# Attention then a Winograd feed-forward: which engine subtracts for the low parts, and which one converts the weights

## The chip, the core and the metric

The kernel runs on one core of one Trainium2 chip. The metric is the device time of the whole program in microseconds (us), lower is better. Each kernel is given by the median of several executions; one more execution was recorded by the hardware profiler and left a trace.

## The reference, cut to what matters

First a linear attention over 8 batches, 8 heads, 576 positions and head width 64, with 128 random features; then a feed-forward layer on the 4608 tokens that result.

```python
def phi(x):
    proj = np.einsum('bhsd,df->bhsf', x, w_phi)
    proj = proj - np.max(np.abs(proj), axis=-1, keepdims=True)
    return np.concatenate([np.exp(proj), np.exp(-proj)], axis=-1)
q_p, k_p = phi(q), phi(k)
kv = np.einsum('bhsf,bhsd->bhfd', k_p, v)
z = np.sum(k_p, axis=2)
attn = np.einsum('bhsf,bhfd->bhsd', q_p, kv) / (np.einsum('bhsf,bhf->bhs', q_p, z)[..., None] + 1e-06)
x = attn.transpose(0, 2, 1, 3).reshape(4608, 512)
h = x @ w_in                                    # 512 x 2048
sp = np.where(h > 20.0, h, np.log1p(np.exp(np.minimum(h, 20.0))))
out = (h * np.tanh(sp)) @ w_out                 # 2048 x 512
```

All is fp32. The weights `w_in` and `w_out` reach the device as 64-bit words, and the kernel turns them into pairs of fp32 numbers itself: this is the weight conversion that the change is about.

## The kernel before, in words

**Attention.** It runs in 36 units of 512 (token, head pair) columns, for k and for q. Per unit TensorE (PE) projects into PSUM; VectorE (DVE) takes the maximum (L199) and subtracts it (L200); ScalarE (ACT) takes the exponentials; PE multiplies with v or with the sums; DVE divides (L304 to L306); PE transposes; ACT copies the result out of PSUM, and it is spilled to DRAM (`x_spill`).

**Feed-forward.** There are 72 steps. A step is 512 tokens (a segment, `s`) times 256 columns of the inner width (`fp`, 8 of them). Each step is seven products of one Winograd level, in two parts, `ff_in(n, 0)` with 24 matmuls and `ff_in(n, 1)` with 18 (L369), and the second layer of earlier steps, `ff_out`, twice 12 matmuls (L434). Every number goes through PE as a high and a low part in fp32r. So the operands are split:

- `x_load` fetches a segment's x into `x32` (one buffer), `x_sum` forms Winograd's differences (L344, on GpSimd, POOL), `x_block` makes seven blocks `xc`, the high part by a cast on ACT (L352) and the low part by a subtraction on DVE (L353).
- `winograd` (L381, L385, L389, L393, on DVE) adds the products in PSUM into `u`. The second part of `ff_in` overwrites what the first three read, so PE waits for L389 before its 18 matmuls.
- `mish` (ACT) applies the activation, `g_hi` casts the high part (L405, ACT), `g_lo` subtracts for the low part `gl` (L411, on POOL).

**Segments.** The first five groups of 512 tokens (`NFIRST`) are gone through with fp 0 and 1, then again with fp 2 and 3, in segments of two steps; all others in segments of four steps. A new segment needs its own x_load, x_sum and x_block.

**Weight conversion.** 32 pieces of 128 x 512 words ("in" or "out", fp, half k), in `weight_ops`. The first part works on bits: `absolute`, `clamp` (L115), `shift` (L119), `sign` (L123), `scale` (L129). The second is arithmetic: `low` (L133), then for "in" `total` (L145), four `sums` (L152), `hi` (a cast on ACT, L157) and `lo` (L161), and for "out" `hi`, `rest` (L166), `lo_out` (L170). All but `hi` and, for the first eight pieces, `absolute` run on DVE. The first eight pieces (fp 0 and 1) are converted during attention, the other 24 during the feed-forward. Those of fp 4 to 7 are spilled and loaded again when their turn comes.

**Order.** No scheduler decides: each action is entered with a nominal time by `at(time, ...)`, the list is sorted, and every engine gets its instructions in that order and executes them in that order. The conversion before is put into a list of free windows (`free`), each operation with a cost. `begin` is the nominal start of the feed-forward, `FFSTEP = 10.6` the nominal step.

Of the kernel before, what the change touches and what calls it, by code (L numbers as in the profile page):

```python
# [44 lines left out]
def attention_then_mish(ctx, tc, qT, kT, va, w_phi, w_in, w_out, out):  # L45
# [52 lines left out]
    def weight_ops(kind, fp, k, quiet):  # L98

        key = (kind, fp, k)  # L100

# [33 lines left out]
        def place():
# [200 lines left out]
    def x_sum(s, i):  # L336
        x32 = xT[s][0]
        if i == 0:
            xT[s].append(ffn.tile([P, 4, 2, CH], F32, tag="xs4", name=f"xs4_{s}", bufs=1))
# [4 lines left out]
        nc.gpsimd.tensor_tensor(o, a, b, op=ALU.subtract)  # L344
# [63 lines left out]
    def g_lo(n):  # L408
        gl = ffn.tile([P, 4, CH], F32R, tag="gl", name=f"gl_{n}", bufs=2)
        eng = nc.vector if n == len(steps) - 1 else nc.gpsimd  # L410
        eng.tensor_tensor(gl, u_live.pop(n)[3], g_live[n][0].bitcast(F32), op=ALU.subtract)  # L411
# [188 lines left out]
```

## Time and profile before

| what | value |
|---|---|
| median of 3 runs | 1144.0 us (1140.62 to 1147.89) |
| the profiled execution, its own time | 1138.37 us |
| its span, from first to last instruction | 1136.6 us |
| mean granted TensorE clock | 0.980 |
| busy: PE, DVE, ACT, POOL | 1064.7, 750.4, 493.7, 299.8 us |
| first h matmul of step 0 (start of the feed-forward) | 295.73 us |

The profile gives for each engine how long it was busy and which instruction ended its idle time. Shares over the whole span hide that this program has stages with different limits, so the stretches are looked at one by one: attention up to 296 us, and the feed-forward after it.

### The profile page before, as it was taken

The page shows a single profiled execution, that of the slowest core. Times are in us where ns is not written, and L with a number is a line of the kernel's source. Part 1 is how long each engine was busy: PE and PEld are TensorE (multiplying, and loading weights), DVE is VectorE, ACT ScalarE, POOL GpSimd, SP SyncE. Part 2 cuts the span into 40 slices and gives each one's busy share as a digit, 9 for nine tenths or more (in the row PEclk, how much of TensorE's full clock was granted, in tenths as well). Part 3 has the DMA queues.
Part 4 walks back from the last instruction along what each step waited for, and adds up shares of the span by engine and source line. Part 5 has one row for each costly group of instructions (what it writes and reads, how often), then busy time and mean ns, then how long its engine had stood idle before and what let it go on. Part 6 is the DMA issues. An engine that isn't in the chain of part 4 may idle for free.

```text
span 1136.6 us, 25710 instructions
## 1 busy us (share of the span) xinstructions
PE 1064.7 (94%) x11200; PEld 964.7 (85%) x11200; DVE 750.4 (66%) x1178; ACT 493.7 (43%) x811; POOL 299.8 (26%) x169
## 2 busy tenths in 40 slices
PE   7999999999888888888898999999999999999998
PEld 6899888998767777777787889999999999999997
DVE  4999999887668899899998863143244244244342
ACT  4667666666435355333333343243233233323331
POOL 0000000001134344433323323324324324324411
PEclk9999999999998899889998999999999999999999
DMA  4545545443223235545653521852320320320321
GB/s 146 188 149 163 191 137 171 131 142 128 71 84 111 93 112 176 176 183 188 201 201 104 200 71 41 300 185 109 112 76 37 111 87 26 112 94 20 110 74 38
DMA packets 64160, 143.45 MB, mean 126 GB/s; under 512 B 5040, under 2 KB 28720, under 8 KB 60464
## 3 DMA queue, kind: packets, MB, share of 16 engines
q1 hardware_dynamic: 64048, 141.81, 36.5%
q8 instruction: 88, 1.44, 0.5%
q14 instruction: 24, 0.20, 0.1%
HBM read 96.70 MB, written 45.09 MB: 125 GB/s over the span
## 4 chain that ended last, share of the span: by engine, by line
PE 47%; DVE 20%; issue 3%; ACT 2%; DMA 1%; POOL 0%; DVEq 0%; ACTq 0%; SPq 0%; POOLq 0%
PE h L369 24%; PE o L434 23%; DVE xc L353 2%; DVE w_in L152 2%; DVE w_in L145 1%; DVE w_in L119 1%; DVE u L393 1%; DVE t_in L133 1%; DVE w_out L123 1%; DVE w_in L123 1%; DVE wst_in L161 1%; DVE u L385 1%; DVE u L389 1%; DVE w_out L110 1%; DVE t_in L129 1%
## 5 line engine op out<-in xcount | busy, mean ns | idle before, releaser
L369 PEld LDWEIGHTS h<-xc,win 128*128 128x128 f32 x3024 | 390.5, 196 | 61.6 <-issue 18.1
L369 PE MATMUL h<-xc,win 128*128 128x256 f32 x3024 | 397.5, 288 | 46.0 <-DVE u L389 45.4
L434 PE MATMUL o<-wout,gh 128*128 128x512 f32 x1152 | 362.0, 396 | 2.9 <-ACT gh L405 2.9
L411 POOL TENSOR_TENSOR gl<-u,gh 128x1024 fp32r<-128x1024 f32 x71 | 173.3, 2441 | 512.2 <-ACT gh L405 450.8
L434 PEld LDWEIGHTS o<-wout,gh 128*128 128x128 f32 x1152 | 210.4, 192 | 39.8 <-ACT gh L405 3.1
L434 PE MATMUL o<-wout,gl 128*128 128x512 f32 x576 | 226.0, 392 | 1.9 <-POOL gl L411 1.7
L344 POOL TENSOR_TENSOR xs<-x 128x512 f32<-128x512 f32 x46 | 64.4, 1399 | 307.3 <-DMA x<-x_spill 282.4
L374 ACT COPY p<-h 128x256 f32<-128x256 f32 x72 | 26.8, 373 | 265.9 <-PE h L369 265.9
L381 DVE TENSOR_TENSOR u<-h,p 128x256 f32<-128x256 f32 x72 | 30.4, 422 | 167.5 <-ACT p L374 167.5
L434 PEld LDWEIGHTS o<-wout,gl 128*128 128x128 f32 x576 | 109.4, 190 | 27.4 <-POOL gl L411 3.2
L393 DVE TENSOR_TENSOR u<-h,u 128x512 f32<-128x512 f32 x72 | 49.4, 686 | 107.1 <-ACT u L398 104.1
L398 ACT ACTIVATE u<-h 128x256 f32<-128x256 f32 x72 | 27.6, 384 | 153.6 <-PE h L369 145.8
L353 DVE TENSOR_TENSOR xc<-x,xc 128x512 fp32r<-128x512 f32 x69 | 75.0, 1114 | 23.9 <-ACT xc L352 23.9
L208 PE MATMUL kvps<-v,e_k 128*64 128x65 f32 x2560 | 83.2, 224 | 5.0 <-ACT e_k L238 4.2
L208 PEld LDWEIGHTS kvps<-v,e_k 128*64 128x64 f32 x2560 | 79.5, 140 | 6.2 <-ACT e_k L238 4.7
L208 PE MATMUL num<-kv,e_q 128*64 128x65 f32 x2304 | 77.6, 223 | 2.6 <-ACT e_q L282 2.4
L208 PEld LDWEIGHTS num<-kv,e_q 128*64 128x64 f32 x2304 | 71.1, 137 | 8.6 <-ACT e_q L282 4.1
L405 ACT CAST gh<-u 128x1024 fp32r<-128x1024 f32 x72 | 75.6, 1050 | 2.2
L282 ACT ACTIVATE e_q<-dt 128x512 f32<-128x512 f32 x144 | 75.1, 612 | 0.1
L237 ACT ACTIVATE e_k<-e_k 128x1024 f32<-128x1024 f32 x36 | 38.1, 1058 | 78.6 <-DVE e_k L200 78.6
L344 POOL TENSOR_TENSOR xs<-x,xs 128x512 f32<-128x512 f32 x46 | 63.9, 1389 | 1.8
L353 DVE TENSOR_TENSOR xc<-xs,xc 128x512 fp32r<-128x512 f32 x92 | 63.2, 718 | 1.0 <-ACT xc L352 1.0
(60 smaller groups left out, 1113.1 us busy)
## 6 DMA issues: line engine op xcount, KB each, us to landing
x<-x_spill SPq DMA_DIRECT2D x46, 512.0 KB, 5.6
o_part<-part SPq DMA_DIRECT2D x14, 1024.0 KB, 4.8
part<-o_part SPq DMA_DIRECT2D x14, 1024.0 KB, 7.5
v<-va SPq DMA_DIRECT2D x32, 325.0 KB, 3.4
kraw<-kT SPq DMA_DIRECT2D x36, 256.0 KB, 3.9
qraw<-qT SPq DMA_DIRECT2D x36, 256.0 KB, 3.9
x_spill<-xs SPq DMA_DIRECT2D x36, 256.0 KB, 2.7
out<-part SPq DMA_DIRECT2D x36, 256.0 KB, 2.0
```

Source lines behind the costliest of these rows:

```text
L208: nc.tensor.matmul(ps[rows], lhsT[:, rows], rhs[h], start=start, stop=stop, skip_group_check=True)
L237: nc.scalar.activation(e[:, :, 1, :], e[:, :, 0, :], AF.Exp)
L282: nc.scalar.activation(e[:, s, :], ps, AF.Exp, scale=2.0 * s - 1.0)
L344: nc.gpsimd.tensor_tensor(o, a, b, op=ALU.subtract)
L353: nc.vector.tensor_sub(blk[:, 1], src, blk[:, 0].bitcast(F32))
L369: nc.tensor.matmul(ps, w, x, start=(i in (0, 2) and m == 0), stop=(m == 5), skip_group_check=True)
L381: nc.vector.tensor_tensor(u2, ps[:, 0, 1], u_live[n][0], op=ALU.add)
L393: nc.vector.tensor_tensor(u[:, 1:3], ps[:, 1], u2.unsqueeze(1).broadcast_to([P, 2, CH]), op=ALU.add)
L398: nc.scalar.activation(u[:, 0], h_live[n][:, 0, 0], AF.Mish)
L405: nc.scalar.copy(gh, u_live[n][3])
L411: eng.tensor_tensor(gl, u_live.pop(n)[3], g_live[n][0].bitcast(F32), op=ALU.subtract)
L434: nc.tensor.matmul(ps, g, w, start=(first and f == k == 0), stop=(last and f == 1 and k == 2))
```

## The change

Three things. (1) `gl` (L415 in the changed file) and the four differences of x per segment (L349) run on VectorE. The third difference is now written in place into `x32`, so that their tile has three slots instead of four. (2) In the weight conversion VectorE keeps the operations on bits; the arithmetic part (`sums`, `lo`, `rest` and `lo_out` in the same manner as `total` below) runs on GpSimd. There `low` becomes two instructions, a multiplication by a constant into the unused half of `w8` (L135) and a product (L137). The pieces are no longer put into free windows but follow each other at fixed distances: the operations on bits 5.0 ahead of the arithmetic, and between pieces a pause of EARLY = 22.0 during attention, SOON = 0.0 for the eight pieces of fp 2 and 3, LATER = 9.0 for the other 16. (3) `NFIRST` is 4 instead of 5, which makes 22 segments of 23; the steps stay 72. Beside these, the tile `wst` moves to another pool, the tile `xs` has two buffers of three, and within the feed-forward `x_block` and `gl` stand 1.4 and 0.9 later in nominal time.

```diff
+EARLY, SOON, LATER = 22.0, 0.0, 9.0
-NFIRST = 5
+NFIRST = 4
...
     def weight_ops(kind, fp, k, quiet):
+        eng = nc.gpsimd
...
         def low():
+            f = piece[key][1][:, 4:8].rearrange("p b m -> p (b m)")
+            nc.gpsimd.tensor_scalar(f, piece[key][0][:, 0], 2.0 ** -52, None, op0=ALU.mult)
             t = piece[key][2]
-            nc.vector.scalar_tensor_tensor(t, piece[key][0][:, 0], 2.0 ** -52, t, op0=ALU.mult, op1=ALU.mult)
+            nc.gpsimd.tensor_tensor(t, f, t, op=ALU.mult)
...
         def total():
-            nc.vector.tensor_tensor(w(), w(), piece[key][2], op=ALU.add)
+            eng.tensor_tensor(w(), w(), piece[key][2], op=ALU.add)
...
     def x_sum(s, i):
...
-        o, a, b = ((t1, b12, b11), (t2, b22, t1), (t3, b22, b12), (t4, b21, t2))[i]
-        nc.gpsimd.tensor_tensor(o, a, b, op=ALU.subtract)
+        o, a, b = ((t1, b12, b11), (t2, b22, t1), (b12, b22, b12), (t4, b21, t2))[i]
+        nc.vector.tensor_tensor(o, a, b, op=ALU.subtract)
...
     def g_lo(n):
-        eng = nc.vector if n == len(steps) - 1 else nc.gpsimd
-        eng.tensor_tensor(gl, u_live.pop(n)[3], g_live[n][0].bitcast(F32), op=ALU.subtract)
+        nc.vector.tensor_tensor(gl, u_live.pop(n)[3], g_live[n][0].bitcast(F32), op=ALU.subtract)
...
-    window, clock = 0, free[0][0]
+    clock = 6.0
     for i, pc in enumerate(pieces):
-        at(clock - 9.0, weight_load, *pc)
-        for cost, op in weight_ops(*pc, i >= 4 * 2):
-            while clock + 0.5 * cost > free[window][1]:
-                window += 1
-                clock = free[window][0]
+        quiet = i >= 8
+        if i == 8:
+            clock = max(clock, begin + 5.0)
+        at(clock - 12.0, weight_load, *pc)
+        bits, sums = weight_ops(*pc, quiet)
+        for delay, op in bits:
+            at(clock - 5.0 + delay, op)
+        for cost, op in sums:
             at(clock, op)
             clock += cost
+        clock += EARLY if i < 8 else SOON if i < 16 else LATER
```

The order shows what this does to the queues. First VectorE in attention, about the second piece. Before, the operations of one piece stand between those of the units, and go on over several units (w_in and t_in are the piece, m, e, pp of the attention unit):

```order
L123 SCALAR_TENSOR_TENSOR w_in_1_978<-words_in_1_741,w_in_1_978 128x512
L129 TENSOR_SCALAR t_in_1_1048<-w_in_1_978 128x512
L199 TENSOR_REDUCE m_k_1078<-pp_k_1057 128x8
L200 TENSOR_TENSOR e_k_1077<-pp_k_1057,m_k_1078 128x2x512
L133 SCALAR_TENSOR_TENSOR t_in_1_1048<-words_in_1_741,t_in_1_1048 128x512
L145 TENSOR_TENSOR w_in_1_978<-w_in_1_978,t_in_1_1048 128x512
```

Of the changed program, the same piece on VectorE:

```order
L117 TENSOR_SCALAR w_in_1_847<-w_in_1_847 128x512
L204 TENSOR_REDUCE m_q_894<-pp_q_787 128x8
L205 TENSOR_TENSOR e_q_893<-pp_q_787,m_q_894 128x2x512
L121 TENSOR_SCALAR w_in_1_847<-w_in_1_847 128x512
L125 SCALAR_TENSOR_TENSOR w_in_1_847<-words_in_1_746,w_in_1_847 128x512
L131 TENSOR_SCALAR t_in_1_906<-w_in_1_847 128x512
```

These four are all of the piece that VectorE still does in attention; the arithmetic stands on GpSimd, which has nothing else there.

Second, VectorE in steps 2 to 4 of the feed-forward, before: most of one piece stands between the last block xc, the adds u of step 4, and the piece's end.

```order
L353 TENSOR_TENSOR xc_6_5592<-xs_2_5448,xc_6_5592 128x512
L115 TENSOR_SCALAR w_in_1_5513<-w_in_1_5513 128x512
L119 TENSOR_SCALAR w_in_1_5513<-w_in_1_5513 128x512
L123 SCALAR_TENSOR_TENSOR w_in_1_5513<-words_in_1_5424,w_in_1_5513 128x512
L129 TENSOR_SCALAR t_in_1_5600<-w_in_1_5513 128x512
L133 SCALAR_TENSOR_TENSOR t_in_1_5600<-words_in_1_5424,t_in_1_5600 128x512
L145 TENSOR_TENSOR w_in_1_5513<-w_in_1_5513,t_in_1_5600 128x512
L381 TENSOR_TENSOR u_4_5635<-h_5602,p_4_5628 128x256
L385 TENSOR_TENSOR u_4_5639<-h_5602,u_4_5635 128x256
L389 TENSOR_TENSOR u_5657<-h_5602,u_4_5639 128x256
L152 TENSOR_TENSOR w_in_1_5513<-w_in_1_5513 128x128 x4
L161 TENSOR_TENSOR win_5481<-w_in_1_5513,win_5481 128x896
```

Of the changed program, VectorE from the adds of step 3 on: gl, one piece's five operations on bits, and the blocks xc between them. The differences of x (L349, four) stand in the step before and in the one after.

```order
L386 TENSOR_TENSOR u_3_5534<-h_5505,p_3_5530 128x256
L390 TENSOR_TENSOR u_3_5538<-h_5505,u_3_5534 128x256
L394 TENSOR_TENSOR u_5553<-h_5505,u_3_5538 128x256
L415 TENSOR_TENSOR gl_5556<-u_5456,gh_5536 128x1024
L112 TENSOR_SCALAR w_in_0_5559<-words_in_0_5500 128x512
L358 TENSOR_TENSOR xc_0_5563<-x_2_5436,xc_0_5563 128x512
L117 TENSOR_SCALAR w_in_0_5559<-w_in_0_5559 128x512
L121 TENSOR_SCALAR w_in_0_5559<-w_in_0_5559 128x512
L358 TENSOR_TENSOR xc_1_5569<-xs_2_5466,xc_1_5569 128x512
L125 SCALAR_TENSOR_TENSOR w_in_0_5559<-words_in_0_5500,w_in_0_5559 128x512
L358 TENSOR_TENSOR xc_2_5593<-xs_2_5466,xc_2_5593 128x512
L131 TENSOR_SCALAR t_in_0_5597<-w_in_0_5559 128x512
```

Third, GpSimd in the same steps, before: the last difference of segment 2, gl of two steps, and the first differences of segment 3.

```order
L344 TENSOR_TENSOR xs_2_5448<-x_2_5417,xs_2_5448 128x512
L411 TENSOR_TENSOR gl_5521<-u_5438,gh_5517 128x1024
L411 TENSOR_TENSOR gl_5641<-u_5535,gh_5637 128x1024
L344 TENSOR_TENSOR xs_3_5664<-x_3_5632 128x512
L344 TENSOR_TENSOR xs_3_5664<-x_3_5632,xs_3_5664 128x512
```

Of the changed program: one "in" piece, and the first instructions of the next. The last of a piece waits for its cast `hi` on ScalarE.

```order
L135 TENSOR_SCALAR w_in_0_5559<-words_in_0_5500 128x512
L137 TENSOR_TENSOR t_in_0_5597<-w_in_0_5559,t_in_0_5597 128x512
L149 TENSOR_TENSOR w_in_0_5559<-w_in_0_5559,t_in_0_5597 128x512
L156 TENSOR_TENSOR w_in_0_5559<-w_in_0_5559 128x128 x4
L165 TENSOR_TENSOR win_5694<-w_in_0_5559,win_5694 128x896
L135 TENSOR_SCALAR w_in_1_5688<-words_in_1_5600 128x512
L137 TENSOR_TENSOR t_in_1_5719<-w_in_1_5688,t_in_1_5719 128x512
```

By the order of the changed program VectorE has, from the adds of step 2 to those of step 8: 24 adds, 5 gl, 12 differences, 21 blocks xc and the operations on bits of 8 pieces; from step 8 to step 16: 32 adds, 8 gl, 16 differences, 28 blocks, 12 drains (L446, PSUM added to a tile) and the bits of 4 pieces. GpSimd has the arithmetic of 4 "in" and 4 "out" pieces in the first stretch, of 4 "in" and 1 "out" in the second.

More of the change, by code (lines that the diff above doesn't have):

```diff
@@ L160, in lo @@
             dst = piece[key][3]
-            nc.vector.tensor_sub(dst[:, 1], piece[key][1][:, 1:8], dst[:, 0].bitcast(F32))
+            eng.tensor_sub(dst[:, 1], piece[key][1][:, 1:8], dst[:, 0].bitcast(F32))
             done()
@@ L165, in rest @@
             dst = piece[key][3]
-            nc.vector.tensor_sub(w(), w(), dst[:, 0].bitcast(F32))
+            eng.tensor_sub(w(), w(), dst[:, 0].bitcast(F32))
         def lo_out():
             dst = piece[key][3]
-            nc.vector.tensor_tensor(dst[:, 1], w(), piece[key][2], op=ALU.add)
+            eng.tensor_tensor(dst[:, 1], w(), piece[key][2], op=ALU.add)
             done()
@@ L177, in done @@
                 nc.sync.dma_start(in_spill[fp, k] if kind == "in" else out_spill[fp, k], dst.bitcast(F32))
-        ops = [(0.42 if quiet else 0.1, absolute), (0.42, clamp), (0.42, shift), (0.69, sign), (0.42, scale), (0.69, low)]
+        ops = [(0.0, absolute), (0.9, clamp), (1.35, shift), (1.8, sign), (2.5, scale)]
+        rest_ops = [(2.2, low)]
         if kind == "in":
-            ops += [(0.69, total)] + [(0.29, lambda i=i: sums(i)) for i in range(4)] + [(1.1, hi), (1.08, lo)]
+            rest_ops += [(1.45, total)] + [(0.65, lambda i=i: sums(i)) for i in range(4)] + [(1.6, hi), (2.3, lo)]
         else:
-            ops += [(0.7, hi), (0.69, rest), (0.69, lo_out)]
-        return ops
+            rest_ops += [(1.3, hi), (1.45, rest), (1.45, lo_out)]
+        return ops, rest_ops
     def project(raw, name):
@@ L530, in attention_then_mish @@
         for i in range(4):
-            at(t + 5.5 + 1.2 * i, x_sum, s, i)
+            at(t + 5.5 + 0.7 * i, x_sum, s, i)
         t = t_of(n - 1) if n >= AHEAD + 2 else begin - (30, 3.9)[s]
         for b in range(7):
-            at(t + 3.5 + 0.8 * b, x_block, s, b)
+            at(t + (4.9 if n >= AHEAD + 2 else 3.5) + 0.8 * b, x_block, s, b)
     for n, (s, sc, fp, first, last) in enumerate(steps):
@@ L547, in attention_then_mish @@
         at(after + 1.8, g_hi, n)
-        at(after + 2.8, g_lo, n)
+        at(after + (3.7 if n >= AHEAD else 2.8), g_lo, n)
         out_a = (begin + 0.9, t_of(n + 1) + 2.8, t_of(n + 1) + 7.8)[min(n, 2)]
```

24 lines of the change are left out of this document (6 added, 18 removed).

## The prediction

> **What bounds the kernel now.** I read the page's busy slices first, then the stretches, then who waits for whom, then the rows of single steps.
>
> ```profile
> span 1136.6 us, 25710 instructions
> PE   7999999999888888888898999999999999999998
> DVE  4999999887668899899998863143244244244342
> ```
>
> PE (TensorE) is near full almost everywhere; the weak slices are 8 to 22, and there DVE (VectorE) is full too. From slice 23 on DVE is far from full. So I cut the span where a step of the feed-forward begins:
>
> ```profile
> 326.38 0.40 PE L369 MATMUL h<-xc,win 128*128 128x256 f32 x2
> 406.69 0.28 PE L369 MATMUL h<-xc,win 128*128 128x256 f32 x1
> 513.07 0.40 PE L369 MATMUL h<-xc,win 128*128 128x256 f32 x2
> 672.06 0.40 PE L369 MATMUL h<-xc,win 128*128 128x256 f32 x2
> ...
> 199.00:256.00 57.00, 57.00 (x1348) 54.27 (x1344) 46.78 (x79) 38.50 (x62) 0.00 (x0) 1.00 0.44 137
> 326.40:406.70 80.30, 67.33 (x386) 60.41 (x385) 66.61 (x94) 34.19 (x59) 30.73 (x17) 0.89 0.31 106
> 406.70:513.10 106.40, 89.98 (x530) 80.21 (x529) 97.86 (x137) 43.72 (x75) 43.50 (x24) 0.94 0.47 167
> 513.10:672.10 159.00, 142.19 (x860) 126.49 (x859) 144.97 (x216) 59.44 (x98) 55.92 (x29) 0.97 0.47 161
> 672.10:1124.40 452.30, 452.30 (x2839) 410.12 (x2838) 165.99 (x274) 153.62 (x255) 153.74 (x83) 1.00 0.27 97
> ```
>
> The first four rows are the first matmuls of steps 2, 8, 16 and 29. The others give, per stretch, its length and the busy time of PE, weight load, DVE, ACT, POOL (GpSimd), then the granted clock. After 672 us PE is busy without a gap: a step has 66 matmuls, 2839 / 66 = 43 steps in 452.3 us, **10.52 us a step**. At that rate steps 2 to 7 would take 63.1 us (they take 80.3), 8 to 15 84.2 (106.4), 16 to 28 136.8 (159.0): 61.6 us are lost, all while weights are being converted, with DVE busy 83%, 92% and 91%. What PE waits for:
>
> ```profile
> PE h L369 <- DVE u L389: 45.4, 13, 5.6
> 344.61 4.18 PE L369 MATMUL h<-xc,win 128*128 128x256 f32 x18 [4.67 <-DVE u L389]
> ```
>
> 13 waits for the third add of DVE; after such a gap the 18 matmuls run slower as well (the granted clock is 0.89 to 0.97 in these stretches, 1.00 after them). DVE bounds them, with its own work and with something else:
>
> ```profile
> 646.25 1.42 POOL L344 TENSOR_TENSOR xs<-x 128x512 f32<-128x512 f32 x1 [1.00 <-DMA x<-x_spill]
> 647.75 1.36 POOL L344 TENSOR_TENSOR xs<-x,xs 128x512 f32<-128x512 f32 x1
> 649.07 1.48 POOL L344 TENSOR_TENSOR xs<-x 128x512 f32<-128x512 f32 x1
> 650.51 1.47 POOL L344 TENSOR_TENSOR xs<-x,xs 128x512 f32<-128x512 f32 x1
> 655.40 2.41 POOL L411 TENSOR_TENSOR gl<-u,gh 128x1024 fp32r<-128x1024 f32 x1 [3.41 <-ACT gh L405]
> ...
> 646.44 1.52 DVE L110 TENSOR_SCALAR w_out<-words_out 128x512 uint32<-128x512 uint32 x1
> 648.00 1.40 DVE L115 TENSOR_SCALAR w_out<-w_out 128x512 f32<-128x512 f32 x1
> 649.43 1.40 DVE L119 TENSOR_SCALAR w_out<-w_out 128x512 uint32<-128x512 uint32 x1
> 650.75 0.68 DVE L393 TENSOR_TENSOR u<-h,u 128x512 f32<-128x512 f32 x1
> 655.87 2.48 DVE L353 TENSOR_TENSOR xc<-x,xc 128x512 fp32r<-128x512 f32 x1 [0.23 <-ACT xc L352]
> 658.27 1.88 DVE L353 TENSOR_TENSOR xc<-xs,xc 128x512 fp32r<-128x512 f32 x3
> 663.09 0.41 DVE L110 TENSOR_SCALAR w_out<-words_out 128x512 uint32<-128x512 uint32 x1
> 663.54 0.43 DVE L115 TENSOR_SCALAR w_out<-w_out 128x512 f32<-128x512 f32 x1
> 664.00 0.43 DVE L119 TENSOR_SCALAR w_out<-w_out 128x512 uint32<-128x512 uint32 x1
> 664.46 0.69 DVE L123 SCALAR_TENSOR_TENSOR w_out<-words_out,w_out 128x512 uint32<-128x512 uint32 x1
> 665.19 0.43 DVE L129 TENSOR_SCALAR t_out<-w_out 128x512 uint32<-128x512 uint32 x1
> ```
>
> The same operations take 0.41, 0.43, 0.43 us with POOL idle and 1.52, 1.40, 1.40 while POOL runs: one of DVE for one of POOL. A block xc that takes 0.63 (three in 1.88) took 2.48 beside a gl. The add L393, with an input in PSUM, kept its 0.68. So **each us of POOL costs DVE part of a us** where DVE works from SBUF: 3.05 of 4.26 us (0.72) over the first three, 1.85 of 2.41 (0.77) over the gl; DVE isn't always at such an operation, so I take two thirds of POOL's busy time. It fits: without it (20.5 of 66.6) DVE would have had 46 us in steps 2 to 7.
>
> The Trainium skill, "SBUF — State Buffer", section "Who interferes with whom", states this as a lock: whichever of the two issues first holds the shared ports for its whole instruction and the other fully blocks, and a VectorE operation with two inputs in SBUF is among those concerned. The trace agrees (2.48 against 0.63 us). By that rule gl and the differences of x come under the lock too once they are on VectorE, which speaks against that part of the change.
>
> **The change, part by part.** In **attention** the unit's rhythm can be read from one row per unit (units 2, 22 and 30 of 36):
>
> ```profile
> 39.45 1.21 DVE L199 TENSOR_REDUCE m_q<-pp_q 128x8 f32<-128x1024 f32 x1
> 200.49 1.21 DVE L199 TENSOR_REDUCE m_q<-pp_q 128x8 f32<-128x1024 f32 x1
> 260.19 1.21 DVE L199 TENSOR_REDUCE m_q<-pp_q 128x8 f32<-128x1024 f32 x1
> ```
>
> Up to 200 us, with eight pieces converted on DVE, a unit takes 161.04 / 20 = 8.05 us; after them 59.70 / 8 = 7.46, with PE busy for all of the stretch 199 to 256 and DVE for 46.78 of 57.00. Twenty units at the faster rate save 11.8 us. Four operations on bits stay, 0.43 + 0.43 + 0.69 + 0.43 = 2.0 us a piece, 16 us in all. DVE has 10.2 us free in 8 units, 1.3 a unit, but a piece's four come close together; I let each of the eight bursts cost PE 0.35 us. POOL's arithmetic beside it hits little: DVE's inputs there are in PSUM. **-9 us** (bounds -12 and 0). The sums of x for the first two segments (2.5 us each) fall into the tail of attention and cost nothing there as long as DVE waits for PE; without that cover 5.
>
> For the feed-forward I need prices on the other engine:
>
> ```profile
> L411 DVE TENSOR_TENSOR gl<-u,gh 128x1024 fp32r<-128x1024 f32 x1 | 1.2, 1226 | 2.0 <-ACT gh L405 2.0
> L385 DVE TENSOR_TENSOR u<-h,u 128x256 f32<-128x256 f32 x72 | 30.5, 424 | 2.5
> masks.py:199 POOL TENSOR_SCALAR_AFFINE_SELECT ident<-ident 128x128 f32<-128x128 f32 x1 | 0.3, 292 | 0.1
> 687.99 2.40 POOL L411 TENSOR_TENSOR gl<-u,gh 128x1024 fp32r<-128x1024 f32 x1 [8.12 <-ACT gh L405]
> 690.35 1.29 POOL L344 TENSOR_TENSOR xs<-x 128x512 f32<-128x512 f32 x1
> x<-x_spill SPq DMA_DIRECT2D x46, 512.0 KB, 5.6
> ```
>
> On DVE: a gl 1.23; the four adds of a step 3 x 0.42 + 0.68 = 1.96; a difference of x like a block xc of its size, 0.63; a drain like L393, 0.68; the bits of a piece 0.41 + 0.43 + 0.43 + 0.69 + 0.43 = 2.39. On POOL 512 columns take 1.29 and 1024 2.40, so 128 about 0.46 and 896 about 2.12. The multiplication by a constant (L135) isn't in the trace: at least the 0.29 of the 128-column select, at most the 2.40 of the 1024 columns, since its input skips every second word of 1024; I take 1.29, the row of its width. An "in" piece is then 3 x 1.29 + 4 x 0.46 + 2.12 = 7.8 us of POOL, an "out" piece 4 x 1.29 = 5.2.
>
> The Trainium skill, "GPSIMD Engine Reference", section "Engine selection", advises VectorE for elementwise work and calls one-input operations on GpSimd roughly line-rate. Its section "Elementwise — side-by-side cycle accounting" has 769 ns for a tight loop over 512 elements; estimated from that page L135 would take 0.77, and the sum below would be 5 us less. No run here shows it yet.
>
> - **Steps 2 to 7** (eight pieces, no pause between them). DVE: 6 x 1.96 + 5 x 1.23 + (12 + 21) x 0.63 + 8 x 2.39 = 57.8. POOL: 4 x 7.8 + 4 x 5.2 = 52.0, two thirds of it on DVE: 34.7. DVE idled 13.7 us here before, partly for casts that now stand on POOL's side; a difference of x now waits on DVE for its DMA (5.6 us from issue, and the issue waits for the last block of the segment before), which I put at 1 us a segment: 8 idle. Sum 100.5 against 80.3: **+20 us**.
> - **Steps 8 to 15** (four "in", one "out"). DVE: 8 x 1.96 + 8 x 1.23 + (16 + 28) x 0.63 + 12 x 0.68 + 4 x 2.39 = 71.0; POOL 36.4, of it 24.3; idle 6 (8.5 before). Sum 101.3 against 106.4: **-5 us**.
> - **Steps 16 to 28.** Eight pieces, three segments: DVE 13 x (1.96 + 1.23) + 33 x 0.63 + 4 x 0.68 + 8 x 2.39 = 84, plus two thirds of POOL's 52: 119 of PE's 136.8. PE bounds, but in the three steps that carry seven blocks (7.6 us with adds and gl) bits and POOL's lock come on top, 13 us against 10.52: 7 us lost instead of 22.2. **-15 us**.
> - **From step 29 on** PE was busy throughout and stays so: 0. That POOL frees DVE there is hidden by PE.
>
> Sum: -9 + 20 - 5 - 15 = **-9 us**. The profiled execution took 1138.4 us in all (1136.6 of span and 1.8 around it), so 1129.4; it lay 0.5% below the median of the runs, 1144.0, and with that ratio I say **1135 us**. About 1% is what a measurement of this kernel can tell from no change.
>
> **The rivals.**
>
> A. *The lock costs little.* POOL's instructions are shorter (0.46 to 2.1 instead of 2.4) and its chain waits for bits and casts; were one third of POOL's time to fall on DVE, steps 2 to 7 take 83 (+3), 8 to 15 89 (-17), the third stretch -18, attention -12: -44, **1100 us**. Against it: the three ratios above.
>
> B. *Attention gains nothing.* The bursts of bits make PE wait as the whole pieces did: -9 becomes 0, the sum 0, **1144 us**. For it: a burst of 2.0 us exceeds the 1.3 that a unit has free; against it: units without conversion run at 7.46.
>
> C. *Slower: DVE and POOL in lockstep.* In steps 2 to 7 POOL's pieces follow without pause and nearly all of DVE's new work there is from SBUF: 33 differences and blocks, 5 gl, 40 on bits. If every us of POOL falls on DVE, steps 2 to 7 take 118 (+38), 8 to 15 113 (+7), the third stretch -10, attention -9: +26, **1170 us**. Each tenth of the share is 5.2 + 3.6 us; the gain is gone at 0.77, and from 0.9 on the kernel is slower by over 1%. For it: the 0.72 and 0.77 are close; against it: POOL pauses for each cast on ACT. The Trainium skill's rule above (first come, the other fully blocks) describes this case.
>
> **How the numbers follow.** Forecast 0.47, A 0.15, B 0.18, C 0.20. Range 1108 to 1165: A's and C's far halves, 0.08 and 0.11, stay outside; the unknown L135, at 0.29 or 2.40, moves the forecast by 14 us down (21 pieces x 1.00 x 2/3) or 10 up (the 13 pieces up to step 15 x 1.11 x 2/3), inside it. Faster by over 1%: A and under half of the forecast, 0.36. Within 1%: the rest of the forecast, most of B, the near end of C, 0.42. Slower: 0.22.
>
> **What would show it.** Right: units of about 7.5 us up to 200 us; steps 2 to 7 about 100 us with DVE near 92% busy and POOL over 50; steps from 16 on at 10.5 us but for some; xc or gl on DVE far above 0.63 and 1.23 where POOL runs. Wrong: a unit of 8 us (B); steps 2 to 7 at 85 or 115 (A, C); L135 far from 1.3; PE waiting for POOL's weights at step 8; ACT held by a cast that waits for POOL, with its copy p behind it.

## The result, and the profile after

The changed kernel takes **1110.4 us** (median of 4 runs, 1109.84 to 1111.28) against 1144.06 (1140.62 to 1147.89): ratio 0.9706, 95% interval 0.9674 to 0.9738. It is 34 us faster; forecast were 9. The profiled execution took 1111.28 us, its span is 1109.5. The two traces differ by less than the medians, 27.1 us in span (1136.6 and 1109.5): of the kernel before, an execution 0.5% under the median was profiled, and of the changed kernel the longest of the four. All stretches below are of the traces.

The first lines of the page, the busy slices of PE, DVE and POOL (GpSimd):

```profile
span 1109.5 us, 25630 instructions
...
PE   7899999999888889999999999999999999999998
...
DVE  4788878888858987898846757545545545545543
...
POOL 0222211111027766543425443000000000000000
```

PE's weak slices are now 11 to 15 (11 to 20 and 22 before), and POOL is busiest just there and behind. The stretches are cut at the first matmul of steps 2, 8, 16 and 29 again; the columns are the length, then busy PE, weight load, DVE, ACT, POOL and the granted clock. The first row is a part of attention:

```profile
57.00:199.00 142.00, 138.92 (x3256) 130.69 (x3254) 120.43 (x205) 95.36 (x153) 32.49 (x31) 1.00 0.48 155
...
329.60:411.60 82.00, 68.45 (x386) 59.32 (x385) 71.83 (x93) 36.39 (x63) 57.69 (x45) 0.92 0.35 122
411.60:504.10 92.50, 86.42 (x529) 76.52 (x528) 79.48 (x122) 40.55 (x69) 47.46 (x37) 0.99 0.53 189
504.10:645.10 141.00, 138.18 (x859) 123.78 (x858) 98.85 (x148) 55.07 (x91) 61.39 (x49) 1.00 0.37 127
645.10:1097.40 452.30, 452.30 (x2839) 410.08 (x2838) 234.91 (x372) 154.94 (x258) 19.24 (x13) 1.00 0.29 103
```

Steps 2 to 7 take 82.0 us (80.3 before), 8 to 15 92.5 (106.4), 16 to 28 141.0 (159.0), and from 29 on a step still takes 10.52. So the whole gain of the trace lies in steps 8 to 28: 13.9 + 18.0 us. Step 0 starts at 297.7 us (295.7), so attention gained nothing. PE's wait for the third add, 45.4 us before, is now

```profile
L374 PE MATMUL h<-xc,win 128*128 128x256 f32 x3024 | 392.3, 285 | 20.2 <-DVE u L394 11.9
```

The lock that the prediction rests on can be added up from the rows of DVE: of each instruction its duration less the shortest of the same line and shape. This **excess** is 25.1, 11.0 and 17.2 us in the three stretches, 0.42, 0.23 and 0.28 of POOL's busy time there (59.0, 48.2 and 61.4 us, summed over its rows). Before the change it was 21.0, 28.9 and 37.6 us, 0.68, 0.66 and 0.67 of POOL's. (An instruction of DVE begins some 0.07 us before the one ahead of it has ended, so the durations of its rows add up to more than its busy time: 77.8 us for 71.8 in steps 2 to 7.)

Of the 87.5 us before, 42.7 lay on the operations on bits, 31.9 on the arithmetic and 12.4 on the blocks xc. Now bits have 9.6, nearly all of it in steps 2 to 7, blocks 24.8, and the differences and gl 17.8. So the conversion, which bore most of the lock before, now bears little of it. Why the share fell can be read in one stretch of a piece, POOL's rows first, then DVE's (start, duration):

```profile
383.76 1.87 POOL L135 TENSOR_SCALAR w_out<-words_out 128x512 f32<-128x512 uint32 x1
388.71 1.27 POOL L137 TENSOR_TENSOR t_out<-w_out,t_out 128x512 f32<-128x512 f32 x1 [3.08 <-DVE t_out L131]
389.94 2.26 POOL L170 TENSOR_TENSOR w_out<-w_out,wout 128x512 f32<-128x512 f32 x1
...
386.43 0.41 DVE L117 TENSOR_SCALAR w_out<-w_out 128x512 f32<-128x512 f32 x1
386.88 0.43 DVE L121 TENSOR_SCALAR w_out<-w_out 128x512 uint32<-128x512 uint32 x1
387.34 0.69 DVE L125 SCALAR_TENSOR_TENSOR w_out<-words_out,w_out 128x512 uint32<-128x512 uint32 x1
388.13 0.43 DVE L131 TENSOR_SCALAR t_out<-w_out 128x512 uint32<-128x512 uint32 x1
388.48 0.42 DVE L386 TENSOR_TENSOR u<-h,p 128x256 f32<-128x256 f32 x1
388.93 0.42 DVE L390 TENSOR_TENSOR u<-h,u 128x256 f32<-128x256 f32 x1
389.39 0.42 DVE L394 TENSOR_TENSOR u<-h,u 128x256 f32<-128x256 f32 x1
389.73 1.33 DVE L415 TENSOR_TENSOR gl<-u,gh 128x1024 fp32r<-128x1024 f32 x1
390.98 1.50 DVE L112 TENSOR_SCALAR w_out<-words_out 128x512 uint32<-128x512 uint32 x1
```

Three things are in it. POOL stands still for 3.08 us while DVE does the bits of the piece it waits for, so they take 0.41 to 0.69, as they do with POOL idle. POOL's L137 then runs beside the three adds from PSUM, which keep their 0.42. And gl, which began 0.2 us ahead of POOL's L170, takes 1.33, while it is POOL's instruction that takes 2.26 instead of 1.29; only the operation behind gl, L112, pays (1.50 for 0.42). The first-come rule of the Trainium skill, "SBUF — State Buffer", "Who interferes with whom", agrees with this last pair: the one that started second was the one drawn out.

### The profile page after: what moved, and what is told of

It is laid out like the page before. It is cut to its first block, busy times and chain, and to the rows that moved or that the text cites. A ratio compares the mean times of both kernels' runs of the same rounds, so it can differ in the third digit from the quotient of the medians.

```text
span 1109.5 us, 25630 instructions
## 1 busy us (share of the span) xinstructions
PE 1057.6 (95%) x11200; PEld 958.3 (86%) x11200; DVE 749.3 (68%) x1166; ACT 489.0 (44%) x804; POOL 245.6 (22%) x198
## 4 chain that ended last, share of the span: by engine, by line
PE 52%; DVE 12%; DMA 2%; ACT 2%; POOL 2%; issue 2%; SPq 0%; DVEq 0%; POOLq 0%; ACTq 0%
PE o L438 27%; PE h L374 25%; DVE xc L358 5%; DMA x<-x_spill 2%; DVE xs L349 1%; DVE gl L415 1%; POOL w_in L156 1%; ACT gh L410 1%; DVE u L398 1%; DVE part L446 1%; DVE w_in L125 0%; ACT u L405 0%; POOL t_in L137 0%; DVE w_in L117 0%; POOL w_in L149 0%
## 5 line engine op out<-in xcount | busy, mean ns | idle before, releaser
L374 PEld LDWEIGHTS h<-xc,win 128*128 128x128 f32 x3024 | 383.8, 193 | 37.6 <-issue 15.1
L374 PE MATMUL h<-xc,win 128*128 128x256 f32 x3024 | 392.3, 285 | 20.2 <-DVE u L394 11.9
L415 DVE TENSOR_TENSOR gl<-u,gh 128x1024 fp32r<-128x1024 f32 x72 | 93.0, 1292 | 29.1 <-ACT gh L410 29.1
L358 DVE TENSOR_TENSOR xc<-x,xc 128x512 fp32r<-128x512 f32 x88 | 75.1, 871 | 11.4 <-ACT xc L357 11.2
L204 DVE TENSOR_REDUCE m_k<-pp_k 128x8 f32<-128x1024 f32 x36 | 44.0, 1222 | 40.6 <-PE pp_k L198 40.3
L405 ACT ACTIVATE u<-u 128x768 f32<-128x768 f32 x72 | 61.1, 849 | 3.0 <-DVE u L398 3.0
L358 DVE TENSOR_TENSOR xc<-xs,xc 128x512 fp32r<-128x512 f32 x66 | 55.5, 861 | 2.0 <-ACT xc L357 2.0
```

The costliest lines, as they stand in the source:

```text
L204: nc.vector.tensor_reduce(m, ps, axis=AX.X, op=ALU.max, apply_absolute_value=True)
L358: nc.vector.tensor_sub(blk[:, 1], src, blk[:, 0].bitcast(F32))
L374: nc.tensor.matmul(ps, w, x, start=(i in (0, 2) and m == 0), stop=(m == 5), skip_group_check=True)
L405: nc.scalar.activation(u[:, 1:4], u[:, 1:4], AF.Mish)
L415: nc.vector.tensor_tensor(gl, u_live.pop(n)[3], g_live[n][0].bitcast(F32), op=ALU.subtract)
```

## The experiments

Three theories were set against each other. **Theory 1**, the prediction's own: DVE gains because arithmetic of the conversion left it, less the lock's share. **Theory 2**: the fixed distances between pieces are the gain. **Theory 3**: gl and the differences of x are; off GpSimd, they no longer lock DVE out. Theory 4, one segment less, stood beside them. Each ratio is to runs of the kernel before on the same chip (medians 1141.3 to 1144.7 us); the start of step 0 and the lengths of the stretches, in us, are from the traces:

| kernel | median, us | ratio to before, 95% | step 0 at | 2 to 7 | 8 to 15 | 16 to 28 |
|---|---|---|---|---|---|---|
| before | 1144.06 | | 295.7 | 80.3 | 106.4 | 159.0 |
| changed | 1110.39 | 0.9706 (0.9674 to 0.9738) | 297.7 | 82.0 | 92.5 | 141.0 |
| changed, gl on POOL | 1135.64 | 0.9938 (0.9910 to 0.9967) | 296.6 | 84.1 | 100.5 | 154.3 |
| changed, differences on POOL | 1128.52 | 0.9870 (0.9811 to 0.9928) | 296.1 | 88.6 | 95.8 | 148.5 |
| changed, both on POOL | 1146.40 | 1.0021 (1.0000 to 1.0042) | 298.3 | 91.4 | 104.2 | 154.9 |
| changed, five first segments | 1113.89 | 0.9739 (0.9681 to 0.9798) | 296.5 | 81.2 | 91.5 | 145.1 |
| changed, arithmetic on DVE | 1102.88 | 0.9648 (0.9588 to 0.9708) | 306.2 | 70.6 | 92.8 | 137.2 |
| before, gl and differences on DVE | 1190.34 | 1.0419 (1.0393 to 1.0445) | 295.8 | 72.7 | 102.1 | 158.8 |
| the same, gl 0.9 later | 1104.74 | 0.9657 (0.9619 to 0.9695) | 294.8 | 67.3 | 95.8 | 150.3 |
| changed, gl 0.9 earlier | 1202.91 | 1.0527 (1.0478 to 1.0576) | 296.1 | 81.4 | 106.0 | 157.7 |
| arithmetic on POOL in attention only | 1093.14 | 0.9567 (0.9543 to 0.9591) | 295.6 | 71.2 | 92.5 | 137.3 |
| changed, bits spread in attention | 1103.88 | 0.9655 (0.9627 to 0.9684) | 288.6 | 79.3 | 97.7 | 140.1 |
| changed, bits ahead | 1109.61 | 0.9711 (0.9688 to 0.9734) | 296.2 | 80.6 | 91.1 | 141.6 |
| POOL in attention only, bits spread | 1088.93 | 0.9524 (0.9483 to 0.9564) | 290.3 | 71.9 | 92.5 | 139.3 |

Step 0 starts anywhere from 295.6 to 298.3 us in the traces of kernels with the changed kernel's attention, so a difference of under 3 us in that column is read as none.

**1. Undo gl.**

```diff
 def g_lo(n):
-    nc.vector.tensor_tensor(gl, ...)
+    eng = nc.vector if n == len(steps) - 1 else nc.gpsimd
+    eng.tensor_tensor(gl, ...)
```

> The changed kernel with gl back on GpSimd (the last step's excepted, as before). Theory 1, 'the lock's share': GpSimd costs VectorE only where the two are independent; the conversion's chain on GpSimd is serial with VectorE's bits and so costs little, but gl is independent of both and costs 0.7 of its 2.40 us where it ran on VectorE for 1.23, and it queues with the chain. 27 gl in steps 2 to 28: VectorE +12 us, GpSimd +65 us on top of 167; steps 2 to 7 at 92 (82), 8 to 15 at 98 (92.5), 16 to 28 at 147 (141): about 1130. Theory 2, 'pacing': the gain is that pieces follow at fixed distances, and gl's place does not matter: 1107 to 1114. Theory 3, 'gl and the sums are the gain': all of the 27 us of the feed-forward come from taking them off GpSimd: 1132 to 1145 with gl alone, as gl is 65 of the 108 us that were taken off.

1135.6 us: 25 us of the gain are gone, as theory 3 expected (1132 to 1145) and a little more than theory 1 did (about 1130). The stretches lose 2, 8 and 13 us; theory 1 had put the loss elsewhere (10, 5.5 and 6). Theory 2, by which the place of gl does not matter, is out as the whole cause. PE's rows of steps 2 to 28 show it waiting on both sides, for DVE's adds and blocks and for POOL's gl:

```profile
PE h L374 <- DVE u L394: 22.3, 13, 7.0
PE h L374 <- DVE xc L358: 10.3, 13, 1.5
PE o L439 <- POOL gl L416: 8.7, 8, 1.7
```

**2. Undo the differences of x.**

```diff
 def x_sum(s, i):
-    nc.vector.tensor_tensor(o, a, b, op=ALU.subtract)
+    nc.gpsimd.tensor_tensor(o, a, b, op=ALU.subtract)
```

> The changed kernel with the four differences of x per segment back on GpSimd (the third still in place). 33 of them stand in steps 2 to 28: 21 us off VectorE, 43 us onto GpSimd. Theory 1 (the lock's share): at 0.7 of 43 us the lock costs VectorE 30 us for 21 us saved, and the differences queue behind the conversion's chain, in steps 2 to 7 above all: 1116 to 1122. Theory 2 (pacing): 1107 to 1114. Theory 3 (gl and the sums are the gain): 43 of 108 us, so about 11 us of 27: 1118 to 1124. Without any of them, since VectorE no longer waits for the load of x with its whole queue behind it (8 us of such waits in steps 8 to 15): 1100 to 1106.

1128.5 us, 18 more than the changed kernel and more than any theory expected. One cost that they left out stands in POOL's waits: the differences wait for the load of x, and with them the conversion behind them in POOL's order, 29.5 us in 7 waits. That this is the whole of the miss is not shown.

```profile
POOL xs L349 <- DMA x<-x_spill: 29.5, 7, 8.6
```

In the changed kernel the wait stands on DVE, with less behind it (steps 8 to 15, then 16 to 28):

```profile
DVE xs L349 <- DMA x<-x_spill: 8.1, 4, 3.1
DVE xs L349 <- DMA x<-x_spill: 1.9, 1, 1.9
```

**3. Undo both.** The edits of 1 and 2 together.

> The changed kernel with gl and the differences of x both back on GpSimd, so that of the change only the move of the arithmetic, the pacing and the first group of four are left. Theory 3 (gl and the sums are the gain, the move of the arithmetic a loss): the two losses measured alone, 25 and 18 us, add up, or more, since gl, differences and conversion then queue on one engine (108 us on top of 167 in 315 us): 1148 to 1175. If the two share one cause that is paid once: 1135 to 1145.

1146.4 us, ratio 1.0021: of the three parts of the change, the move of the arithmetic, the pacing and the group of four together bring **nothing**; 25 and 18 us would have made 1153, so 7 of them are shared. The median lies between the two ranges that were expected, 1.6 us under theory 3's and 1.4 above the other. Theory 3 holds so far. What each of the three parts brings alone this run cannot tell.

**4. Undo the group of four.**

```diff
-NFIRST = 4
+NFIRST = 5
```

> The changed kernel with a first group of five segments, as before: 23 segments instead of 22, so 4 differences and 7 blocks more on VectorE (7 us) and one more load of x, but two more steps before the weights of fp 2 are due. Theory 4, 'one segment less': each new segment in the stretch where VectorE bounds costs its 7 us and a wait for x of 2 us: 1117 to 1121. Theory 1 and 2: the conversion of eight pieces spreads over 8 steps instead of 6, steps 2 to 9 lose as much as 2 to 7 did: 1108 to 1114. If steps 2 to 7 are bound by the due time of the weights of fp 2 (PE waiting for GpSimd's chain), faster: 1100 to 1106.

1113.9 us. The intervals overlap (0.9681 to 0.9798 and 0.9674 to 0.9738), so the segment's worth, 3.5 us by the medians, isn't told from nothing.

**5. The arithmetic on VectorE.**

```diff
 def weight_ops(kind, fp, k, quiet):
-    eng = nc.gpsimd
+    eng = nc.vector
...
     def scale():
-        t = ffn.tile([P, 512], F32, tag="t", ...)
+        t = piece[key][1][:, 4:8].rearrange("p b m -> p (b m)")
...
     def low():
-        nc.gpsimd.tensor_scalar(f, piece[key][0][:, 0], 2.0 ** -52, None, op0=ALU.mult)
-        nc.gpsimd.tensor_tensor(t, f, t, op=ALU.mult)
+        nc.vector.scalar_tensor_tensor(t, piece[key][0][:, 0], 2.0 ** -52, t, op0=ALU.mult, op1=ALU.mult)
```

> The changed kernel with the arithmetic of the conversion on VectorE again (low as the one instruction it was, t in the unused half of w8), everything else and the pacing as changed. GpSimd is then idle but for its start. Theory 1 (the lock's share): VectorE takes 3.6 us more for an 'in' piece and 2.1 for an 'out' piece, 68 us for 24 pieces, and gets back the lock's 52 us; in attention 23 us more on VectorE: steps 2 to 7 about the same (82), 8 to 15 +3, 16 to 28 +2, attention +3: 1113 to 1122. Theory 2 (pacing) 1107 to 1113. Theory 3 (gl and the sums are the gain, since GpSimd idle means no lock): 1105 to 1112. If the move of the arithmetic is what made the kernel faster: 1130 or more.

1102.9 us, faster than any theory expected, nearest to theory 3 (1105 to 1112). In the feed-forward it is worth more than the median says: steps 2 to 7 fall to 70.6 us, 16 to 28 to 137.2, the excess of DVE to 0.7, 0.8 and 1.2 us. In steps 2 to 7 DVE's own work (its rows at their shortest, added up) grows from 52.7 to 73.4 us, and the stretch is 11.4 us shorter all the same: the 25 us of excess are gone, and DVE is idle for 6.1 us instead of 10.2. Attention loses 8.5 us (step 0 at 306.2): there the arithmetic on DVE delays the units. On POOL it costs DVE next to nothing there: the excess in all of attention is 1.5 us in the changed kernel and 1.4 here, where POOL does none of it. The next experiment takes the better place for each.

**6. The arithmetic on POOL in attention only.**

```diff
 def weight_ops(kind, fp, k, quiet):
-    eng = nc.gpsimd
+    eng = nc.vector if quiet else nc.gpsimd
```

with `t` and `low` as in experiment 5 for the pieces of the feed-forward (`quiet`), and as in the changed kernel for the first eight.

> The changed kernel with the arithmetic of the 24 pieces of the feed-forward on VectorE, and that of the first eight pieces on GpSimd as changed. In attention VectorE's operands lie in PSUM and the lock costs 1 us, so GpSimd is free help there; in the feed-forward it is not. Theory 3 with that distinction: step 0 at 298 as in the changed kernel (306 with all arithmetic on VectorE), steps 2 to 7 at 71, 8 to 15 at 93, 16 to 28 at 137: 1092 to 1097. If the gain of the run with all arithmetic on VectorE came from a cooler or shifted attention instead: 1100 to 1110.

1093.1 us, as expected, ratio 0.9567, clear of the changed kernel's interval. The rows of steps 2 to 7, 8 to 15 and 16 to 28:

```profile
327.00:398.20 71.20, 64.19 (x386) 57.02 (x385) 64.60 (x129) 35.72 (x62) 0.00 (x0) 0.95 0.40 136
398.20:490.70 92.50, 87.89 (x529) 78.36 (x528) 82.44 (x154) 41.32 (x71) 0.00 (x0) 0.96 0.53 192
490.70:628.00 137.30, 137.30 (x860) 123.71 (x859) 102.88 (x189) 55.09 (x91) 0.00 (x0) 1.00 0.38 130
```

With POOL idle, DVE is busy 64.6 us in the first stretch, against 71.8 in the changed kernel, although it now does the arithmetic of the same pieces; in the last PE is busy without a gap. So **moving the arithmetic to GpSimd cost the feed-forward 14.5 us** (315.5 against 301.0 for steps 2 to 28) and saved attention 10.6 (step 0 at 295.6 against 306.2 in experiment 5). The edit also takes away the single tile `t`, for which DVE had to wait for POOL; that wait was 2.7 us in all of steps 2 to 28.

**7. gl and the differences alone.** On the kernel before, its windows and its five segments unchanged:

```diff
-        nc.gpsimd.tensor_tensor(o, a, b, op=ALU.subtract)
+        nc.vector.tensor_tensor(o, a, b, op=ALU.subtract)
...
-        eng = nc.vector if n == len(steps) - 1 else nc.gpsimd
-        eng.tensor_tensor(gl, ...)
+        nc.vector.tensor_tensor(gl, ...)
```

> The kernel before with only gl and the four differences of x moved to VectorE: conversion, windows and five first segments as before. GpSimd is then idle in the feed-forward, so the lock is gone (it cost VectorE 87 us in steps 2 to 28), and VectorE takes 33 us for 27 gl and 25 us for 40 differences: 29 us less of VectorE in a stretch that lost 61.6 us to it. Theory 3 (gl and the sums are the gain): 1105 to 1118, attention as before (step 0 at 296), steps 2 to 28 at 318 or less (346 before, 315 in the changed kernel). Theory 1 (the move of the arithmetic is a gain of its own): 1122 to 1135. Theory 2 (pacing is the gain): 1138 to 1146.

1190.3 us, **slower than before**, against all three theories. Steps 2 to 7 gained 8 us and 8 to 15 gained 4; the loss is where nobody looked, from step 29 on. The 43 steps there take 515.5 us, 12.0 each:

```profile
661.50:1177.00 515.50, 462.51 (x2841) 406.71 (x2840) 220.87 (x357) 153.92 (x255) 0.00 (x0) 1.00 0.24 84
...
917.06 0.42 DVE L385 TENSOR_TENSOR u<-h,u 128x256 f32<-128x256 f32 x1
918.43 1.23 DVE L410 TENSOR_TENSOR gl<-u,gh 128x1024 fp32r<-128x1024 f32 x1 [0.95 <-ACT gh L405]
919.58 0.42 DVE L389 TENSOR_TENSOR u<-h,u 128x256 f32<-128x256 f32 x1
...
PE h L369 <- DVE u L389: 53.0, 43, 1.2
```

gl stands between the second and the third add. It waits 0.95 us for its cast on ACT, takes 1.23, and the third add, for which PE waits, comes behind it. PE waits in all 43 steps. In the changed kernel the three adds follow each other and gl comes after:

```profile
912.06 0.42 DVE L390 TENSOR_TENSOR u<-h,u 128x256 f32<-128x256 f32 x1
912.52 0.42 DVE L394 TENSOR_TENSOR u<-h,u 128x256 f32<-128x256 f32 x1
913.43 1.23 DVE L415 TENSOR_TENSOR gl<-u,gh 128x1024 fp32r<-128x1024 f32 x1 [0.49 <-ACT gh L410]
```

That is the 0.9 of nominal time that the diff adds to gl. Two runs tested it from both sides.

**8. The same, gl 0.9 later.** To the edits of 7:

```diff
-        at(after + 2.8, g_lo, n)
+        at(after + (3.7 if n >= AHEAD else 2.8), g_lo, n)
```

> The kernel before with gl and the differences of x on VectorE, as in the run of part 1 alone, and gl 0.9 later in nominal time, as the change has it. In that run gl stood between the second and the third add of the next step, waited there for its cast on ScalarE, and made every step from 29 on 12.0 us long. Theory 'the place of gl': steps from 29 on at 10.52, steps 2 to 7 at 70 to 73, 8 to 15 at 91 to 97, 16 to 28 at 139 to 150, attention as before (296): 1095 to 1118. If gl on VectorE costs a step its 1.5 us wherever it stands (then the changed kernel would have another reason for its 10.52): 1170 or more.

1104.7 us, within the range expected, ratio 0.9657. Steps from 29 on take 10.52 us again, and this kernel, which leaves conversion and windows as they were, beats the before by 40 us: as much as the changed kernel does, or a little more (the intervals overlap).

```profile
325.60:392.90 67.30, 62.60 (x386) 56.17 (x385) 57.65 (x109) 34.09 (x59) 0.00 (x0) 0.97 0.34 116
392.90:488.70 95.80, 87.08 (x530) 77.67 (x529) 88.38 (x162) 43.69 (x75) 0.00 (x0) 0.96 0.53 189
488.70:638.90 150.20, 140.00 (x859) 124.79 (x858) 133.43 (x246) 59.44 (x98) 0.00 (x0) 0.99 0.50 171
638.90:1091.20 452.30, 452.30 (x2839) 410.06 (x2839) 223.35 (x357) 153.68 (x255) 0.00 (x0) 1.00 0.27 97
...
PE h L369 <- DVE u L389: 21.9, 13, 5.5
```

The first row against 80.3 us and 66.6 of DVE: with gl and differences *added* to it, DVE is busy 9 us less, and its excess is 0.7 us instead of 21.0. The last row is PE's wait for the third add in steps 2 to 28, 45.4 us before.

This kernel and that of experiment 5 have gl, the differences and the arithmetic on VectorE alike. What differs is the conversion in free windows or at fixed distances, the group of five or four, the nominal places of the differences and blocks, and where some tiles lie. Their medians cannot be told apart (0.9657 and 0.9648), but their stretches can: with the changed kernel's order steps 2 to 28 take 300.6 us for 313.4, and step 0 starts at 306.2 for 294.8. So the new order is a gain of 13 us in the feed-forward and a loss of 11 in attention; which of its parts makes it is not shown, beyond the 3.5 us of experiment 4, which are not told from nothing.

**9. The changed kernel, gl 0.9 earlier.** The last edit undone.

> The changed kernel with gl at its old nominal time, 0.9 earlier, all else as changed. Theory 'the place of gl': every step from 29 on 1.5 us longer (43 x 1.5 = 65 us), the steps before them 0 to 1.5 us longer: 1170 to 1195, slower than the kernel before. If the place matters only where windows and conversion on VectorE are as before: 1108 to 1116.

1202.9 us, ratio 1.0527. From step 29 on a step takes 12.0 us again, 62 us in all; steps 8 to 28 lose 30 more, which the expectation had put too low. The place of gl is worth 92 us, nearly three times the whole gain.

**10. The bits spread in attention.**

```diff
-    clock = 6.0
+    clock = 36.0
...
-        at(clock - 12.0, weight_load, *pc)
+        at(clock - (12.0 if quiet else 42.0), weight_load, *pc)
...
-            at(clock - 5.0 + delay, op)
+            at(clock - 5.0 + (delay if quiet else 7.4 * bits.index((delay, op)) - 28.0), op)
```

> The changed kernel with the operations on bits of the first eight pieces put one per unit of attention (7.4 us apart, over the five units ahead of the arithmetic; the arithmetic starts 30 us later) instead of 2 us in one unit. If the burst is what keeps attention from gaining (the first q unit at 28.95 us instead of 26.71, units of 7.88 us up to 200 us): units of 7.5 to 7.7, step 0 at 292 to 295, 1104 to 1108. If TensorE itself sets the unit (it was busy 138.9 of 142 us from 57 to 199 us, before as after): step 0 at 296 to 298, 1107 to 1111.

Step 0 starts at 288.6 us, 9 earlier than in the changed kernel and earlier than the 292 to 295 expected, and the median falls to 1103.9 (ratio 0.9655, interval 0.9627 to 0.9684); 5 us are lost again in steps 8 to 15. Rows of the first q unit and of units 2 and 22, first of the changed kernel, then of this one:

```profile
28.95 1.22 DVE L204 TENSOR_REDUCE m_q<-pp_q 128x8 f32<-128x1024 f32 x1
41.65 1.21 DVE L204 TENSOR_REDUCE m_q<-pp_q 128x8 f32<-128x1024 f32 x1
199.30 1.21 DVE L204 TENSOR_REDUCE m_q<-pp_q 128x8 f32<-128x1024 f32 x1
```

```profile
25.95 1.21 DVE L204 TENSOR_REDUCE m_q<-pp_q 128x8 f32<-128x1024 f32 x1
38.15 1.21 DVE L204 TENSOR_REDUCE m_q<-pp_q 128x8 f32<-128x1024 f32 x1
192.18 1.22 DVE L204 TENSOR_REDUCE m_q<-pp_q 128x8 f32<-128x1024 f32 x1
```

3.5 of the 9 us are won by unit 2, where a whole burst had stood ahead of the first q unit; from there to unit 22 a unit takes 7.70 us instead of 7.88 (7.81 to 7.93 in the other traces with the changed kernel's attention). Spread out, the bits now lie beside POOL: the excess in attention grows from 1.5 to 5.5 us, 4.1 of it on `clamp` (L117). The run also moves the first arithmetic 30 us later, which isn't told apart from the spreading.

**11. The bits ahead.** For the pieces of the feed-forward:

```diff
-        at(clock - 12.0, weight_load, *pc)
+        at(clock - (16.0 if quiet else 12.0), weight_load, *pc)
...
-            at(clock - 5.0 + delay, op)
+            at(clock - (9.0 if quiet and delay < 2 else 5.0) + delay, op)
```

> The changed kernel with the first four operations on bits of the 24 pieces of the feed-forward put 4 us earlier in nominal time (their load too), so that they stand beside GpSimd's arithmetic of the piece before, not behind it. Theory 'serial': the lock's share is low (0.42, 0.23, 0.28) because GpSimd waits while VectorE has the bits; now the bits are hit: shares of 0.5 to 0.6, VectorE +8 to +15 us in steps 2 to 28, 1113 to 1122 unless GpSimd's chain, no longer waiting, makes up for it. Rival 'the share is that of the mix': it is low because VectorE's gl and adds are hardly hit whatever the order; shares as they were, and 1105 to 1111 as the chain waits less.

1109.6 us, no change that can be told. The shares rose to 0.47, 0.32 and 0.31 only. Added up over the rows, the bits lay beside POOL for 19.9 us in steps 2 to 7 (13.9 in the changed kernel), and their excess went from 8.7 to 11.6; but in steps 8 to 28 they overlap with POOL for just 4.6 us (0.4 before the edit), so there the edit did not make the case it was meant to. The serial order as the cause of the low share is supported in steps 2 to 7 and not tested behind them.

**12. Both improvements**, experiments 6 and 10 together.

> The kernel with the arithmetic of the first eight pieces on GpSimd and of the other 24 on VectorE, and the operations on bits of the first eight one per unit of attention. If the two gains, 17 and 6.5 us against the changed kernel, are independent: step 0 at 287 to 289, steps 2 to 28 as in the first of them (301): 1084 to 1088. If what attention gains is lost again in steps 8 to 15, as half of it was with the arithmetic on GpSimd (97.7 for 92.5 us): 1089 to 1093.

1088.9 us, ratio 0.9524 (0.9483 to 0.9564): the fastest of all, though its interval overlaps with that of experiment 6 (0.9543 to 0.9591). The gains do not quite add up (1084 to 1088 expected for that). In the trace, which is of the longest of the four executions, attention gained 5.3 us and steps 16 to 28 gave back 2.0.

## Why the prediction was wrong

The time lies in the range, at its lower edge, and the forecast of "no change that can be told" is wrong. In the traces, which the prediction counted in, the change is worth 27.1 us and not 9: attention +2.0 (forecast -9), steps 0 and 1 +1.2 (not priced), 2 to 7 +1.7 (+20), 8 to 15 -13.9 (-5), 16 to 28 -18.0 (-15). So steps 2 to 28 were forecast 30 us too dear and attention 11 us too cheap. That the time still lies in the range is luck: the two errors have opposite signs, and with attention at -9 it would have come out at about 1099, under the range's 1108. By its own steps:

- **What bounds the kernel: right.** DVE, through its own work and the lock, in steps 2 to 28. Two thirds was also the right share for the schedule before (0.66 to 0.68 by the rows). Experiment 8 took POOL's work out of these steps and gave gl and the differences to DVE: DVE's excess fell from 21.0, 28.9 and 37.6 us to 0.7, 1.0 and 1.6, and 32.3 of the 33.1 us by which its span is shorter lie there (313.4 us against 345.7). One line was misread without harm: PE's weak slices before are 11 to 20 and 22, not 8 to 22.
- **The lock's two thirds: the step that failed most.** It came from rows of before in which DVE happened to be at bits and blocks, and was carried to a schedule in which POOL waits for those bits (52.1 us in steps 16 to 28, below) and runs beside adds from PSUM and gl instead. Measured: 0.42, 0.23, 0.28. POOL itself was busy longer than forecast (59.0 and 48.2 us for 52.0 and 36.4), and the lock was less all the same, 25 us for 34.7 in steps 2 to 7 and 11 for 24.3 in 8 to 15. The other terms of these two sums were off as well:

| term, us | steps 2 to 7, forecast | measured | steps 8 to 15, forecast | measured |
|---|---|---|---|---|
| DVE's own work (busy less excess) | 57.8 | 46.7 | 71.0 | 68.5 |
| the lock (excess) | 34.7 | 25.1 | 24.3 | 11.0 |
| DVE idle | 8 | 10.2 | 6 | 13.0 |
| sum | 100.5 | 82.0 | 101.3 | 92.5 |

In steps 2 to 7 the own work was put 11 us too high. Only 17 of the 21 blocks and 35 of the 40 operations on bits began inside the stretch, and the rows overlap by 6.0 us, which only the price of the blocks allowed for. In steps 16 to 28, where PE bounds, 144 became 141.0. POOL's waits in that last stretch:

```profile
POOL t_in L137 <- DVE t_in L131: 31.5, 4, 10.0
POOL t_out L137 <- DVE t_out L131: 20.6, 4, 8.4
```

- **Attention, -9: wrong.** It came out at +2.0, which the variation of step 0 does not tell from nothing. The failed term is the burst of bits at 0.35 us each. From unit 2 to 22 a unit takes 7.88 us and not the 7.46 counted on, 8.4 us more in 20 units with five bursts. Units 22 to 30 took 7.46 before, without any conversion; the new distances put two bursts there, and they take 7.80. Unit 30 begins at

```profile
261.67 1.21 DVE L204 TENSOR_REDUCE m_q<-pp_q 128x8 f32<-128x1024 f32 x1
```

That makes 1.3 to 1.7 us a burst, beside the first one, after which the first q unit begins 2.2 us later than before. It is the mechanism of rival B. With the bits spread, step 0 starts 9.1 us earlier than in the changed kernel, but only 7.1 earlier than before (experiment 10).
- **Rivals A and B were taken as exclusive.** A's stretches (83, 89, -18) are close to 82.0, 92.5 and -18.0, but its 1100 held attention at -12. Over steps 2 to 28 the excess is 53.3 us for 168.6 us of POOL, 0.32: A's third. A with B's attention is 1112, and 1110.4 was measured. C is refuted: no stretch has a share over 0.42, and the differences and gl on DVE did not bring lockstep.
- **From step 29 on, 0: right by luck, through an edit that was not priced.** The 0.9 of nominal time by which gl moves was listed and costed at nothing, and PE named as its cover. Without it these steps take 12.0 us, and the change would have been slower by 5% (experiment 9). The right question was asked of the differences (what stands behind the waiting instruction), not of gl.
- **The prices on GpSimd were right but one.** 512 columns took 1.29 and 128 columns 0.46 in the median, 896 columns 2.2 in the mean; L135 took

```profile
L135 POOL TENSOR_SCALAR w_in<-words_in 128x512 f32<-128x512 uint32 x16 | 26.2, 1639 | 124.3 <-DMA words_in<-w_in 123.7
L135 POOL TENSOR_SCALAR w_out<-words_out 128x512 f32<-128x512 uint32 x16 | 28.2, 1762 | 72.5 <-DMA words_out<-w_out 71.7
```

1.64 and 1.76 us in the mean, inside its bounds and above the 1.29 taken. The 0.77 us estimated from the Trainium skill's "GPSIMD Engine Reference", "Elementwise — side-by-side cycle accounting", is less than half of that; the trace does not agree with it.
- **The parts were never priced apart.** With the prediction's own 34.7 us, the arithmetic of the eight pieces in steps 2 to 7 costs DVE that much from GpSimd, and on DVE itself 22.8 (four 'in' pieces at 0.69 + 0.69 + 4 x 0.29 + 1.08 = 3.62 and four 'out' pieces at 3 x 0.69 = 2.07, by the rows of before with POOL idle). That sum would have shown that two parts of the change work against each other there, as experiments 3 and 6 found.

## What to carry to other kernels

Price each part of a change alone, also against leaving it out: here the sum hid a gain of 40 us (gl and the differences, at their new place) and a loss of 14.5 (the arithmetic in the feed-forward). A share of interference measured in one schedule doesn't carry to another: ask which instructions will stand beside each other, which of them were drawn out beside the other engine in the rows at hand, and which wait for each other anyway. And before an operation is put on an in-order engine, look at the instruction that will stand behind it: 0.9 us of place decided over 92 us of time.
